# k of chunk 2 loaded in blocks, later attention places and an earlier w_in trigger in a fused retention and GELU kernel

## The chip, the cores and the metric

One core of a Trainium2 chip. The metric is the device time of one execution in microseconds, as the median of several runs. All runs told here are of the fast state; a profile lists one execution, and its span is about 1.7 us shorter than the measured time of the same execution (212.0 against 213.73 for the kernel before).

## The reference, cut to what matters

```python
# q, k, v: (4, 8, 768, 64): batch, head, position, head_dim
for t in range(S):
    state = gamma * state + k[:, :, t] (outer) v[:, :, t]
    y[:, :, t] = 0.125 * q[:, :, t] @ state
x = y.transpose(0, 2, 1, 3).reshape(3072, 512)
h = x @ w_in                      # (512, 2048)
out = gelu_tanh(h) @ w_out        # (2048, 512)
```

The recurrence is computed in six chunks of 128 positions, numbered 0 to 5. In a chunk, for each batch: T (q and k transposed), A (k times q, masked), Y (state times q, plus A times v), S (the new state). The two dense layers of a chunk are called M1 (16 units of TensorE work, then GELU on ScalarE) and M2 (16 units). Attention of chunk n+1 is placed between the units of M1 and M2 of chunk n.

## The kernel before

In the code below PO is GpSimd, VE is VectorE, SY is the SP queue (the DMA queue that SyncE issues), and `prep` scales or converts what was loaded. q of chunks 2 to 5 and k of chunks 3 to 5 are loaded in 32-wide blocks, scaled by GpSimd and transposed by VectorE (0.70 to 0.71 us per 128x512 in the trace of before). All other q and k go through TensorE.

```python
BLK = {"q": (2, 3, 4, 5), "k": (3, 4, 5)}

def load_blk(nm, c):                 # 16 DMAs of 64 KB, runs of 128 bytes
    ...
    for j in range(2):
        for dd in range(2):
            for a in range(4):
                nc.sync.dma_start(out=t[p0:p0 + 32, :, a, :], in_=src[j, dd, t0:t0 + 32])

def load(c):                         # everything of a chunk, on the SP queue
    for nm in "qk":
        if c in BLK[nm]:
            load_blk(nm, c)
    for b in range(B):
        for nm in "vk":              # k also in plain rows: S needs it so
            load1(nc.sync, nm, c, b)

def mm_A(c, b):                      # 8 matmuls; lhsT is k, rhs is q, both transposed
    ...
def ev_A(c, b):                      # 2 masked evictions on VectorE
    ...
```

The start, on GpSimd (`k` of batch 2 is the "third k"):

```python
prep1(PO, "k", 0, 1)
prep1(PO, "k", 0, 2)                 # scale k of batch 2
load_w_in(0)
load_w_in(1)                         # first two w_in parts
prep1(PO, "k", 0, 3)
```

The steady stage, for chunks 3 to 5 (n = c + 1; the keys count units of M1, 0 to 15, and M2, 16 to 31):

```python
after = {
    2: [(prep_blk, nm, n, b) for b in range(B) for nm in "qk"],
    6: [(att_T, n, 0)],
    8: [(att_T, n, 1)] + [(prep1, PO, nm, n, b) for b in range(B) for nm in "kv"],
    9: [(load, n + 1)] if n + 1 < NCk else [],
    10: [(att_T, n, 2)],
    12: [(att_AY, n, (), "att", n, (0, 1), None)],   # A of batches 0 and 1
    14: [(att_T, n, 3)],
    17: [(att_AY, n, (), "att", n, (2, 3), None)],   # A of batches 2 and 3
    21: [(att_Y, n)],
    23: [(att_S, n, 0)], 24: [(att_S, n, 1)], 25: [(att_S, n, 2)], 26: [(att_S, n, 3)],
}
```

Of the kernel before, what the change touches and what calls it, by code (L numbers as in the profile page):

```python
# [9 lines left out]
F16 = mybir.dt.float16  # L10
# [6 lines left out]
def kernel(  # L17
# [9 lines left out]
    nc = tc.nc  # L27
    B, H, S, Dh = q.shape
    C = 128
    NCk = S // C  # L30
    NHP = H // 2
# [25 lines left out]
    pre = ctx.enter_context(tc.tile_pool(name="pre", bufs=2 * B))  # L57
    att = ctx.enter_context(tc.tile_pool(name="att", bufs=4))
# [8 lines left out]
    misc = const.tile([128, 32], F32)  # L67
# [5 lines left out]



    BLK = {"q": (2, 3, 4, 5), "k": (3, 4, 5)}

    def ld_all(key):
        if key not in raw:
            raw[key] = ld.tile(  # L80
                [128, B * NHP, 4, 32],
                F32,
                tag=key[0],
                bufs=2 if key[0] == "q32" else 1,
                name=key[0],
            )
        return raw[key]

    def ld_tile(nm, c, b):
        if nm == "q":  # L90
            t = ld_all(("q32", c)).rearrange("p (b hp) a d -> p b (hp a d)", b=B)
            return t[:, b].rearrange("p (h d) -> p h d", h=H)
        if (nm, c, b) not in raw:
            raw[nm, c, b] = ld.tile([128, H, Dh], F32, tag=f"{nm}32", bufs=6, name=f"{nm}32")
        return raw[nm, c, b]

    def load1(eng, nm, c, b):
        eng.dma_start(  # L98
            out=ld_tile(nm, c, b),
            in_=srcs[nm][b, :, c * C:(c + 1) * C, :].rearrange("h p d -> p h d"),  # L100
        )

    def load_blk(nm, c):
        t = ld_all((nm + ("32" if nm == "q" else "T32"), c))
        src = srcs[nm].rearrange("b (hp j) s (dd d) -> j dd s (b hp) d", j=2, dd=2)
# [3 lines that stand above are left out]
                    p0, t0 = (2 * j + dd) * 32, c * C + a * 32  # L109
                    nc.sync.dma_start(  # L110
                        out=t[p0:p0 + 32, :, a, :], in_=src[j, dd, t0:t0 + 32]
                    )

    def load(c):
# [4 lines that stand above are left out]
            for nm in "vk":  # L119
                load1(nc.sync, nm, c, b)  # L120
# [22 lines left out]
    for j in range(2):  # L143
# [3 lines left out]
        out=iden,  # L147
        in_=iden,
# [7 lines left out]
        out=mask.rearrange("p j hp t -> p (j hp) t"),  # L156
        in_=mask.rearrange("p j hp t -> p (j hp) t"),
# [7 lines left out]
        out=misc[:, 0:1], in_=zero[:, 0:1], func=AF.Gelu_apprx_tanh, scale=1.0  # L165
# [15 lines left out]
    blk16 = {}  # L181

    def prep1(eng, nm, c, b):
        t = pre.tile(
            [128, H, Dh], F16, tag=f"{nm}16", bufs=6 if nm == "q" else 2 * B, name=f"{nm}16"
        )
        src = ld_tile(nm, c, b)
        if nm == "v":
            if eng is nc.scalar:
                eng.copy(out=t, in_=src)  # L190
            else:
                eng.tensor_copy(out=t, in_=src)  # L192
        else:
            col = OQ if nm == "q" else OK
            eng.tensor_tensor(  # L195
                out=t,
                in0=src,
                in1=cst[:, col:col + H].unsqueeze(2).broadcast_to([128, H, Dh]),
                op=ALU.mult,
            )  # L200
        h16[nm, c, b] = t

    def prep_blk(nm, c, b):
        key, tag, col = ("q32", "q16", OQT) if nm == "q" else ("kT32", "kT16", OKT)
        t = pre.tile([128, NHP * 4, 32], F16, tag=tag, bufs=6 if nm == "q" else 2, name=tag)
        nc.gpsimd.tensor_tensor(  # L206
            out=t,
            in0=ld_all((key, c))[:, b * NHP:(b + 1) * NHP].rearrange("p hp a d -> p (hp a) d"),
            in1=cst[:, col:col + 16].unsqueeze(2).broadcast_to([128, 16, 32]),
            op=ALU.mult,  # L210
        )
        blk16[nm, c, b] = t

    def pair(t, hp):
        return t[:, 2 * hp:2 * hp + 2]

    qkT = {}
    a_sb = {}
    xT = {}
    pss = {}  # L220

    def copy_on(eng, out, in_):
        if eng is nc.scalar:
            eng.copy(out=out, in_=in_)  # L224
        else:
            eng.tensor_copy(out=out, in_=in_)  # L226
# [5 lines left out]
    def bank(tag, dt=F32, shape=(128, NHP, 128), name="ps"):  # L232
        return psum.tile(list(shape), dt, tag=tag, bufs=BANKS[tag], name=name)

    def mm_T(c, b):
        parts = [(i, nm) for i, nm in enumerate("qk") if c not in BLK[nm]]
        if not parts:
            return
        ps = bank("att", F16, (128, 2, NHP, 128), "qkT_ps")
        for i, nm in parts:  # L240
            for hp in range(NHP):
                nc.tensor.transpose(  # L242
                    out=ps[:, i, hp], in_=pair(h16[nm, c, b], hp), identity=iden
                )
        pss["T", c, b] = ps

    def ev_T(c, b, eng=nc.vector):
        t = att.tile([128, 2, NHP, 128], F16, tag="qkT", name="qkT")
        for i, nm in enumerate("qk"):
            if c in BLK[nm]:  # L250
                nc.vector.transpose(  # L251
                    out=t[:, i].rearrange("p hp t -> p (hp t)"),
                    in_=blk16.pop((nm, c, b)).rearrange("p ha d -> p (ha d)"),
                )
        if ("T", c, b) in pss:
            i0 = sum(c in BLK[nm] for nm in "qk")
            copy_on(eng, t[:, i0:], pss.pop(("T", c, b))[:, i0:])
        qkT[c, b] = t

    def mm_A(c, b):  # L260
        t = qkT[c, b]
# [90 lines left out]
    def att_T(c, *bs):  # L352
        for b in bs:
            mm_T(c, b)
            ev_T(c, b)
# [51 lines left out]
    def load_w_in(n):  # L407
        i, k0, k1 = w_in_part[n]
        nc.gpsimd.dma_start(  # L409
            out=w_in_sb[n],  # L410
            in_=moe_w_in.rearrange("(kc p) (i n) -> p kc i n", p=128, i=NI)[:, k0:k1, i],
        )
# [29 lines left out]
    def moe1(c, fc):  # L442
        h_ps = bank("h", shape=(128, B * C), name="h_ps")
        moe1_mm(c, fc, h_ps, 0, B * C)
        gelu(g_tile(c, fc)[:, fc % 2], h_ps)
# [65 lines left out]
    def run(units, after):  # L511
        for i, u in enumerate(units):
            u()
            for f, *args in after.get(i, ()):
                f(*args)

    VE, AC, PO, SY = nc.vector, nc.scalar, nc.gpsimd, nc.sync
# [10 lines left out]
    load1(AC, "v", 0, 2)  # L528
    prep1(VE, "q", 0, 1)
    prep1(PO, "k", 0, 1)  # L530
    prep1(PO, "k", 0, 2)

    load_w_in(0)
    load_w_in(1)
    prep1(PO, "k", 0, 3)
    for i in range(2, len(w_in_part)):
        load_w_in(i)
# [97 lines left out]
    )  # L635


    for b in range(B):
        load1(SY, "k", 2, b)
    load_blk("q", 2)  # L640
    for rows, o_sb in late:
        nc.sync.dma_start(out=rows, in_=o_sb)
    for b in range(B):
        load1(SY, "v", 2, b)
    for nm in "kqv":
        for b in range(B):
            prep_blk("q", 2, b) if nm == "q" else prep1(PO, nm, 2, b)
    run(
        [
            (lambda fp=fp, t=t: moe1_two(1, fp, *t))  # L650
# [5 lines left out]
            3: [(att_S, 1, 2)],  # L656
            4: [(att_AY, 1, (3,), "o", 1, (), VE)],
            6: [(att_S, 1, 3)],
            8: [(att_T, 2, 0), (load, 3)],
            10: [(att_T, 2, 1)],  # L660
            14: [(att_AY, 2, (), "att", 2, (0, 1), None)],
        },
    )
    run(
        [x for b in range(B) for x in units2(1, b)],
        {
            0: [(att_T, 2, 2), (att_T, 2, 3)],
            3: [(att_AY, 2, (), "att", 2, (2, 3), None)],
            7: [(att_Y, 2)],
            9: [(att_S, 2, 0)],  # L670
            10: [(att_S, 2, 1)],
            11: [(att_S, 2, 2)],
            12: [(att_S, 2, 3)],
        },
    )

# [1 line left out]
    for c in range(2, NCk - 1):  # L678
        n = c + 1
        after = {  # L680
            2: [(prep_blk, nm, n, b) for b in range(B) for nm in "qk"],
            6: [(att_T, n, 0)],
            8: [(att_T, n, 1)] + [(prep1, PO, nm, n, b) for b in range(B) for nm in "kv"],
            9: [(load, n + 1)] if n + 1 < NCk else [],
            10: [(att_T, n, 2)],
            12: [(att_AY, n, (), "att", n, (0, 1), None)],
            14: [(att_T, n, 3)],
            17: [(att_AY, n, (), "att", n, (2, 3), None)],
            21: [(att_Y, n)],
            23: [(att_S, n, 0)],  # L690
            24: [(att_S, n, 1)],
            25: [(att_S, n, 2)],
            26: [(att_S, n, 3)],
        }
        run(
            [(lambda fc=fc: moe1(c, fc)) for fc in range(NF)]
            + [x for b in range(B) for x in units2(c, b)],
            after,
        )
    c = NCk - 1  # L700
# [36 lines left out]
```

## Time and profile before

| | before |
|---|---|
| time, median of 3 runs | 213.74 us (213.12 to 213.77) |
| span of the profiled run | 212.0 us |
| TensorE busy | 204.6 us, 96% |
| TensorE waits after 18.2 us | none |
| matmuls that transpose q or k | 80 |

The page, TensorE's waits and the chain are shown in the prediction. One more view is needed later: the order of loads on the SP queue, which is never idle from 65 to 94 us. The columns are start, duration of the issue, engine queue, line, operation, what, count. The last line is GpSimd scaling the first k block of chunk 3.

```profile
65.04 9.93 SPq L110 DMA_DIRECT2D q<-in_q_dram  x16
75.03 8.77 SPq L110 DMA_DIRECT2D kT<-in_k_dram  x16
...
88.39 1.05 POOL L206 TENSOR_TENSOR kT<-kT,cst 128x512 f16<-128x512 f32 x1
```

The k blocks of chunk 3 were all issued by 83.8 us (the last landed at 86.40), and GpSimd came to them at 88.39 without waiting. A of chunk 3 stood at 96.86, so they were ready far ahead.

### The profile page before, as it was taken

How to read it: one execution, taken by the hardware profiler on the slowest of the kernel's cores; microseconds unless marked ns; L12 is line 12 of the kernel's file. 1: busy time of each engine (PE TensorE's matmuls, PEld its weight loads, DVE VectorE, ACT ScalarE, POOL GpSimd, SP SyncE). 2: the span in 40 equal slices, each digit the busy share in tenths (PEclk: the TensorE clock that was granted, in tenths of full speed). 3: DMA queues.
4: the chain of work that ended last, by engine and by line, in shares of the span. 5: the costliest groups of instructions: out<-in, count | busy, mean ns of one | idle time of the engine just before them, and what ended most of it. 6: DMA issues, size and time to landing. Idle time of an engine off the chain costs nothing.

```text
span 212.0 us, 3873 instructions
## 1 busy us (share of the span) xinstructions
PE 204.6 (96%) x1518; PEld 111.1 (52%) x1518; DVE 89.6 (42%) x162; ACT 84.2 (40%) x141; POOL 94.8 (45%) x116
## 2 busy tenths in 40 slices
PE   7798999999999999999999999999999999999992
PEld 2457444457897465444465444464444464444461
DVE  6677100198618736356544356544356520100000
ACT  2464661255455131466131466131466131565110
POOL 2597300523819517799218699211699201100000
PEclk9999999999999999999999999999999999999999
DMA  6999999999889878998779996799900012100121
GB/s 155 289 251 206 206 203 231 233 246 236 135 229 215 148 170 134 250 222 148 120 154 205 290 183 108 122 186 254 248 0 3 0 49 102 49 0 0 49 102 50
DMA packets 124289, 32.78 MB, mean 155 GB/s; under 512 B 118064, under 2 KB 122416, under 8 KB 124272
## 3 DMA queue, kind: packets, MB, share of 16 engines
q1 hardware_dynamic: 108880, 20.75, 49.5%
q0 software_dynamic: 5600, 8.65, 17.1%
q10 hardware_dynamic: 9792, 3.15, 6.2%
q8 instruction: 12, 0.20, 0.4%
q14 instruction: 5, 0.04, 0.1%
HBM read 30.44 MB, written 6.29 MB: 173 GB/s over the span
## 4 chain that ended last, share of the span: by engine, by line
PE 90%; DMA 7%; POOL 1%; SPq 1%; DVE 0%; issue 0%
PE o_ps L470 40%; PE h_ps L425 39%; DMA w_in<-in_moe_w_in_dram 3%; DMA k<-in_k_dram 3%; PE a_ps L265 3%; PE y_ps L300 3%; PE y_ps L287 2%; PE s_ps L319 2%; PE qkT_ps L242 1%; SPq L98 1%; POOL k L195 0%; POOL w_in L409 0%; DVE o_sb L508 0%; SPq L126 0%
## 5 line engine op out<-in xcount | busy, mean ns | idle before, releaser
L470 PE MATMUL o_ps<-w_out,g 128*128 128x512 f16 (+1 forms) x400 | 88.2, 371 | 0.0
L425 PE MATMUL h_ps<-xT,w_in 128*128 128x512 f16 (+1 forms) x464 | 86.6, 343 | 0.7 <-DMA w_in<-in_moe_w_in_dram 0.7
L440 ACT ACTIVATE g<-h_ps 128x512 f16<-128x512 f32 x96 | 57.3, 597 | 48.2 <-PE h_ps L425 48.1
L425 PEld LDWEIGHTS <-w_in 128*128 128x128 f16 x464 | 44.4, 98 | 38.1 <-DMA w_in<-in_moe_w_in_dram 0.8
L470 PEld LDWEIGHTS <-g 128*128 128x128 f16 x400 | 37.6, 98 | 38.7
L278 DVE TENSOR_TENSOR a_sb<-a_ps,mask 128x512 f16<-128x512 f32 x48 | 30.1, 683 | 17.5 <-PE a_ps L265 17.5
L492 ACT COPY o_sb<-o_ps 128x512 f32<-128x512 f32 x19 | 11.1, 585 | 54.9 <-PE o_ps L470 50.5
L497 POOL DMA_DIRECT2D out_dram<-o_sb x17 | 9.6, 563 | 47.3 <-ACT o_sb L492 37.5
L195 POOL TENSOR_TENSOR k<-k,cst 128x512 f16<-128x512 f32 x23 | 23.7, 1035 | 12.3 <-DMA k<-in_k_dram 12.3
L345 POOL TENSOR_TENSOR stg<-st,cst 128x512 f32<-128x512 f16 x16 | 16.4, 1040 | 10.7 <-DVE st L336 8.9
L206 POOL TENSOR_TENSOR q<-q,cst 128x512 f16<-128x512 f32 x16 | 16.6, 1047 | 5.0 <-DMA out_dram<-o_sb 5.0
L336 DVE TENSOR_TENSOR st<-s_ps,stg 64x256 f16<-64x256 f32 x32 | 13.5, 421 | 7.8 <-PE s_ps L319 7.3
L251 DVE STREAM_TRANSPOSE qkT<-q 128x512 f16<-128x512 f16 x16 | 11.3, 707 | 11.6 <-POOL q L206 11.6
L195 DVE TENSOR_TENSOR q<-q,cst 128x512 f16<-128x512 f32 x8 | 5.9, 739 | 16.0 <-DMA q<-in_q_dram 15.9
L226 DVE CAST xT<-y_ps 128x512 f16<-128x512 f32 x11 | 7.2, 686 | 12.7 <-PE y_ps L300 12.7
L206 POOL TENSOR_TENSOR kT<-kT,cst 128x512 f16<-128x512 f32 x12 | 12.5, 1042 | 0.0
L508 DVE COPY o_sb<-o_ps 128x256 f32<-128x256 f32 x2 | 0.8, 424 | 26.6 <-PE o_ps L470 26.6
L224 ACT CAST xT<-y_ps 128x512 f16<-128x512 f32 x13 | 7.2, 587 | 8.7 <-PE y_ps L300 8.7
L171 PE MATMUL spin_ps<-zero 128*128 128x512 f16 x30 | 9.1, 444 | 1.3 <-DVE zero L139 1.3
L490 DVE COPY o_sb<-o_ps 128x512 f32<-128x512 f32 x4 | 2.8, 691 | 16.4 <-PE o_ps L470 14.7
L251 DVE STREAM_TRANSPOSE qkT<-kT 128x512 f16<-128x512 f16 x12 | 8.4, 700 | 2.6 <-POOL kT L206 2.6
L192 POOL CAST v<-v 128x512 f16<-128x512 f32 x16 | 9.5, 602 | 0.0
(33 smaller groups left out, 97.5 us busy)
## 6 DMA issues: line engine op xcount, KB each, us to landing
v<-in_v_dram SPq DMA_DIRECT2D x22, 256.0 KB, 4.4
k<-in_k_dram SPq DMA_DIRECT2D x20, 256.0 KB, 4.7
out_dram<-o_sb POOLq DMA_DIRECT2D x17, 256.0 KB, 3.2
q<-in_q_dram SPq DMA_DIRECT2D x64, 64.0 KB, 2.6
kT<-in_k_dram SPq DMA_DIRECT2D x48, 64.0 KB, 2.6
w_out<-in_moe_w_out_dram POOLq DMA_DIRECT2D x4, 512.0 KB, 15.8
w_in<-in_moe_w_in_dram POOLq DMA_DIRECT2D x3, 512.0 KB, 9.2
q<-in_q_dram SPq DMA_DIRECT2D x5, 256.0 KB, 5.9
```

What stands on the lines that cost most here:

```text
L192: eng.tensor_copy(out=t, in_=src)
L195: eng.tensor_tensor(out=t, in0=src, in1=cst[:, col:col + H].unsqueeze(2).broadcast_to([128, H, Dh]), op=ALU.mult,)
L206: nc.gpsimd.tensor_tensor(out=t, in0=ld_all((key, c))[:, b * NHP:(b + 1) * NHP].rearrange("p hp a d -> p (hp a) d"), in1=cst[:, col:col + ...
L251: nc.vector.transpose(out=t[:, i].rearrange("p hp t -> p (hp t)"), in_=blk16.pop((nm, c, b)).rearrange("p ha d -> p (ha d)"),)
L278: nc.vector.tensor_tensor(out=s, in0=ps[j], in1=mask[:, j], op=ALU.mult)
L336: eng.tensor_tensor(out=st[sl, :, b, sl], in0=s_ps[sl, :, sl], in1=stg[sl, :, b, sl], op=ALU.add,)
L345: nc.gpsimd.tensor_tensor(out=stg[:, :, b], in0=st[:, :, b], in1=cst[:, OG:OG + NHP].unsqueeze(2).broadcast_to([128, NHP, 128]), op=ALU.mult,)
L425: nc.tensor.matmul(out=out, lhsT=w_in_of(fc, kc), rhs=xT[c][:, kc, t0:t1], start=(kc == 0 and first), stop=(kc == NHP - 1), skip_group_che ...
L440: nc.scalar.activation(out=out, in_=in_, func=AF.Gelu_apprx_tanh, scale=1.0)
L470: nc.tensor.matmul(out=ps[:, n0:n1], lhsT=g_sb[c, fc // 2][:, fc % 2, b * C:(b + 1) * C], rhs=w_out_sb[fc // (NF // NO)][:, fc % (NF // NO ...
L492: nc.scalar.copy(out=o_sb, in_=ps)
L497: eng.dma_start(out=rows, in_=o_sb)
```

## The change

Three things: k of chunk 2 also comes in blocks, so that no TensorE transposes are left after chunk 1; attention of chunks 2 to 5 is placed later, with all q transposed well ahead of k; and w_in is triggered as soon as the third k has landed, before it is scaled. To hold the first two apart, `tr` (the transposes on VectorE) now runs for q and for k separately, GpSimd scales all four q blocks before the four k blocks, and there are four buffers for scaled k blocks instead of two; these lines are not shown.

```diff
-    BLK = {"q": (2, 3, 4, 5), "k": (3, 4, 5)}
+    BLK = {"q": (2, 3, 4, 5), "k": (2, 3, 4, 5)}
@@ start
     prep1(PO, "k", 0, 1)
-    prep1(PO, "k", 0, 2)
+    nc.gpsimd.tensor_copy(out=misc[0:1, 4:5], in_=ld_tile("k", 0, 2)[0:1, 0, 0:1])
     load_w_in(0)
     load_w_in(1)
+    prep1(PO, "k", 0, 2)
     prep1(PO, "k", 0, 3)
@@ loads of chunk 2
-    for b in range(B):
-        load1(SY, "k", 2, b)
     load_blk("q", 2)
+    load_blk("k", 2)
     ...
+    for nm in "vk":
         for b in range(B):
+            load1(SY, nm, 2, b)
+    load(3)
@@ M2 of chunk 1 (keys: units; chunk 2's A used to be at unit 14 of M1 and 3 of M2)
+            1: [(tr, 2, "k", 0, 1)],
+            3: [(att_AY, 2, (), "att", 2, (0, 1), None), (tr, 2, "k", 2, 3)],
+            7: [(att_AY, 2, (), "att", 2, (2, 3), None)],
+            11: [(att_Y, 2)],
+            12: [(att_S, 2, 0)],   ... 15: [(att_S, 2, 3)],
@@ chunks 3 to 5
-            12: A(0, 1)   14: T(3)   17: A(2, 3)   21: Y   23 to 26: S        (shortened)
+            2: [(prep, n, "QKvk"), (tr, n, "q")],
+            15: [(tr, n, "k", 0, 1)],
+            18: [(att_AY, n, (), "att", n, (0, 1), None), (tr, n, "k", 2, 3)],
+            22: [(att_AY, n, (), "att", n, (2, 3), None)],
+            26: [(att_Y, n)],
+            27: [(att_S, n, 0)],   ... 30: [(att_S, n, 3)],
```

More of the change, by code (lines that the diff above doesn't have):

```diff
@@ L204, in prep_blk @@
         key, tag, col = ("q32", "q16", OQT) if nm == "q" else ("kT32", "kT16", OKT)
-        t = pre.tile([128, NHP * 4, 32], F16, tag=tag, bufs=6 if nm == "q" else 2, name=tag)
+        t = pre.tile([128, NHP * 4, 32], F16, tag=tag, bufs=6 if nm == "q" else 4, name=tag)
         nc.gpsimd.tensor_tensor(
@@ L235, in mm_T @@
     def mm_T(c, b):
-        parts = [(i, nm) for i, nm in enumerate("qk") if c not in BLK[nm]]
-        if not parts:
-            return
         ps = bank("att", F16, (128, 2, NHP, 128), "qkT_ps")
-        for i, nm in parts:
+        for i, nm in enumerate("qk"):
             for hp in range(NHP):
@@ L245, in mm_T, with qkT_tile, tr @@
         pss["T", c, b] = ps
+    def qkT_tile(c, b):
+        if (c, b) not in qkT:
+            qkT[c, b] = att.tile([128, 2, NHP, 128], F16, tag="qkT", name="qkT")
+        return qkT[c, b]
     def ev_T(c, b, eng=nc.vector):
-        t = att.tile([128, 2, NHP, 128], F16, tag="qkT", name="qkT")
-        for i, nm in enumerate("qk"):
-            if c in BLK[nm]:
-                nc.vector.transpose(
-                    out=t[:, i].rearrange("p hp t -> p (hp t)"),
-                    in_=blk16.pop((nm, c, b)).rearrange("p ha d -> p (ha d)"),
-                )
-        if ("T", c, b) in pss:
-            i0 = sum(c in BLK[nm] for nm in "qk")
-            copy_on(eng, t[:, i0:], pss.pop(("T", c, b))[:, i0:])
-        qkT[c, b] = t
+        copy_on(eng, qkT_tile(c, b), pss.pop(("T", c, b)))
+    def tr(c, nm, *bs):
+        for b in bs or range(B):
+            nc.vector.transpose(
+                out=qkT_tile(c, b)[:, "qk".index(nm)].rearrange("p hp t -> p (hp t)"),
+                in_=blk16.pop((nm, c, b)).rearrange("p ha d -> p (ha d)"),
+            )
     def mm_A(c, b):
@@ L635, with prep @@
     )
-    for b in range(B):
-        load1(SY, "k", 2, b)
     load_blk("q", 2)
+    load_blk("k", 2)
     for rows, o_sb in late:
         nc.sync.dma_start(out=rows, in_=o_sb)
-    for b in range(B):
-        load1(SY, "v", 2, b)
-    for nm in "kqv":
+    for nm in "vk":
         for b in range(B):
-            prep_blk("q", 2, b) if nm == "q" else prep1(PO, nm, 2, b)
+            load1(SY, nm, 2, b)
+    load(3)
+    def prep(c, nms):
+        for nm in nms:
+            for b in range(B):
+                prep1(PO, nm, c, b) if nm in "kv" else prep_blk(nm.lower(), c, b)
     run(
@@ L658 @@
             6: [(att_S, 1, 3)],
-            8: [(att_T, 2, 0), (load, 3)],
-            10: [(att_T, 2, 1)],
-            14: [(att_AY, 2, (), "att", 2, (0, 1), None)],
+            7: [(prep, 2, "Q")],
+            8: [(tr, 2, "q")],
+            10: [(prep, 2, "Kvk")],
         },
@@ L666 @@
         {
-            0: [(att_T, 2, 2), (att_T, 2, 3)],
-            3: [(att_AY, 2, (), "att", 2, (2, 3), None)],
-            7: [(att_Y, 2)],
-            9: [(att_S, 2, 0)],
-            10: [(att_S, 2, 1)],
-            11: [(att_S, 2, 2)],
-            12: [(att_S, 2, 3)],
+            1: [(tr, 2, "k", 0, 1)],
+            3: [(att_AY, 2, (), "att", 2, (0, 1), None), (tr, 2, "k", 2, 3)],
+            7: [(att_AY, 2, (), "att", 2, (2, 3), None)],
+            11: [(att_Y, 2)],
+            12: [(att_S, 2, 0)],
+            13: [(att_S, 2, 1)],
+            14: [(att_S, 2, 2)],
+            15: [(att_S, 2, 3)],
         },
@@ L680 @@
         after = {
-            2: [(prep_blk, nm, n, b) for b in range(B) for nm in "qk"],
-            6: [(att_T, n, 0)],
-            8: [(att_T, n, 1)] + [(prep1, PO, nm, n, b) for b in range(B) for nm in "kv"],
+            2: [(prep, n, "QKvk"), (tr, n, "q")],
             9: [(load, n + 1)] if n + 1 < NCk else [],
-            10: [(att_T, n, 2)],
-            12: [(att_AY, n, (), "att", n, (0, 1), None)],
-            14: [(att_T, n, 3)],
-            17: [(att_AY, n, (), "att", n, (2, 3), None)],
-            21: [(att_Y, n)],
-            23: [(att_S, n, 0)],
-            24: [(att_S, n, 1)],
-            25: [(att_S, n, 2)],
-            26: [(att_S, n, 3)],
+            15: [(tr, n, "k", 0, 1)],
+            18: [(att_AY, n, (), "att", n, (0, 1), None), (tr, n, "k", 2, 3)],
+            22: [(att_AY, n, (), "att", n, (2, 3), None)],
+            26: [(att_Y, n)],
+            27: [(att_S, n, 0)],
+            28: [(att_S, n, 1)],
+            29: [(att_S, n, 2)],
+            30: [(att_S, n, 3)],
         }
```

## The prediction

> **What bounds the kernel now.** I read four views in this order: the page's busy rows and slices, the waits of TensorE alone, the chain of work that ended last, and the timelines of TensorE and VectorE around one attention block.
>
> From the page:
>
> ```profile
> PE 204.6 (96%) x1518; PEld 111.1 (52%) x1518; DVE 89.6 (42%) x162; ACT 84.2 (40%) x141; POOL 94.8 (45%) x116
> ...
> PE   7798999999999999999999999999999999999992
> ...
> PEclk9999999999999999999999999999999999999999
> ```
>
> TensorE is busy at full granted clock from the fifth slice (about 21 us) to the end, and no other engine reaches half. Busy TensorE is not proof, since ends of matmuls are modelled, so the next view is who TensorE waited for:
>
> ```profile
> PE a_ps L265 <- ACT qkT L224: 1.3, 3, 0.6
> PE spin_ps L171 <- DVE zero L139: 1.3, 1, 1.3
> PE h_ps L425 <- DMA w_in<-in_moe_w_in_dram: 0.7, 1, 0.7
> ```
>
> These three rows are all there is. All lie in the first 18.2 us; afterwards TensorE waits for nothing. So after 18 us only two things change the time: matmuls removed, at their issue spacing, and new waits. The chain (start, duration, what) shows the spacing and where the start-up ends:
>
> ```profile
> 2.36 6.42 DMA k<-in_k_dram
> 8.78 0.07 issue
> 8.85 1.04 POOL k L195
> 9.89 0.84 POOL w_in L409
> 10.72 7.36 DMA w_in<-in_moe_w_in_dram
> 18.09 0.05 issue
> 18.14 0.61 PE h_ps L425 x4
> ...
> 60.65 0.22 PE qkT_ps L242 x4
> ...
> 62.62 0.22 PE qkT_ps L242 x4
> ...
> 68.74 0.45 PE qkT_ps L242 x8
> 69.18 2.59 PE o_ps L470 x12
> ```
>
> The start-up is third k lands, GpSimd scales it, GpSimd triggers w_in, w_in lands at 18.09, first full-rate work. Later, four transposes take 0.22 us of TensorE (55 ns each) and four 512-column matmuls 2.59/3 = 0.863 us (216 ns each).
>
> [...] I count removed work at the spacing, not at the 219 ns that the groups give as the mean of one 128-column matmul. [...] the trace shows the vector form at 0.70 us per 128x512. [...] the DMA share in the slices is 9 throughout from 5 to 53 us. [...] 1 MB of q in 32-wide blocks (128 B runs) took the SP queue 9.59 us, 1 MB of k in plain rows (256 B runs) 4.66 us.
>
> **The change part by part.**
>
> *k of chunk 2 in blocks.* Removes 4 batches x 4 = 16 TensorE transposes: 16 x 55 ns = 0.88 us, all on the setting path (the rows above: 0.22 + 0.22 + 0.45 = 0.89). It also removes 4 PSUM copies of about 0.40 us on VectorE and adds 4 vector transposes of 0.70 us, 4 GpSimd multiplies of 1.04 us and 1 MB of block loads, about 9 us of SP queue. None of those is on the path unless late. *Gain 0.88 us.*
>
> *Later attention.* Moves no work in or out of TensorE, the same matmuls run a few units later. It only matters through waits. The critical distance is between the two A groups: in the before loop there were 5 units between them, now 4. From the timelines of chunk 3:
>
> ```profile
> 96.86 0.62 PE L265 MATMUL a_ps<-qkT 64*128 64x128 f16 x16
> ...
> 97.29 2.48 DVE L278 TENSOR_TENSOR a_sb<-a_ps,mask 128x512 f16<-128x512 f32 x4 [3.09 <-PE a_ps L265]
> 99.69 0.70 DVE L251 STREAM_TRANSPOSE qkT<-q 128x512 f16<-128x512 f16 x1
> 100.31 0.67 DVE L251 STREAM_TRANSPOSE qkT<-kT 128x512 f16<-128x512 f16 x1
> ```
>
> VectorE starts evicting 0.43 us after A starts, needs 2.48 us for four evictions, then 0.62 us per transpose pitch: the second one ends 4.12 us after A's start (100.98 - 96.86). In the changed loop the two k transposes of batches 2 and 3 stand exactly there. TensorE comes back for batch 2 after 0.55 + 4 x 0.865 + 0.11 (the small lag seen after each A group) = 4.12 us and for batch 3 at about 4.39. Batch 2 is ready at about 3.5, batch 3 at 4.12. So the wait is nil, but batch 3 has only some 0.25 us to spare. *Expected 0 to 0.1 us for each of four chunks; I put 0.1 in all.*
>
> *Loads of chunk 2.* SP starts q blocks at 44.65 instead of k's plain rows: q until 54.3, k blocks (9 us) until about 63.5, landing 2.6 us later, about 66. GpSimd then needs 2 x 1.04 us and VectorE 0.70 us until batch 1's k is transposed: 69. M2 of chunk 1 begins at 67.87 - 0.55 (A moved out) - 0.44 (transposes) = 66.9 and A of chunk 2 follows 4 units later, at 70.3. Slack a bit over 1 us. Afterwards all loads are some 9 us later in the SP queue: chunk 3's loads end at about 102 instead of 93.6. Its v is first read by TensorE at unit 26, about 109, and GpSimd's last v conversion is due at about 104. Later chunks regain 3.5 us each (stage 31.8 us, loads 28.3 us). *0, or a wait of up to 1 us once.*
>
> *w_in earlier.* GpSimd now does a 1x1 copy instead of the 1.04 us multiply ahead of the trigger (the only 1x1 copy in the trace took 0.18 us), so w_in is triggered about 0.85 us earlier. But the k multiply of batch 2 comes after two triggers of together 1.64 us: it ends at about 11.7 instead of 9.89. TensorE transposed that k at 11.14, so the batch-2 chain slips about 0.5 us. Following it through (transpose, PSUM copy, A, eviction, last y) the last y before the w_in wait ends at about 17.9 instead of 17.48. It waited for w_in until 18.14. So even a w_in that lands 0.85 us earlier gives only 18.14 - 17.9 = 0.25 us. If the DMA engines are simply full, w_in lands at 18.1 as before and the gain is 0. *Gain 0.15 us.*
>
> Sum: 0.88 + 0.15 - 0.1 = 0.93, say 1.0 us with the three before runs lying at 213.12 to 213.77: 213.74 - 1.0 = 212.7 us.
>
> **The rivals.** (a) *A new wait takes the gain back*: k transposes of batches 2 and 3 queue behind the evictions on VectorE. For it: the distance of 4 units leaves only 0.25 us. Against: the before durations, taken from the same overlap with GpSimd, just fit. With 0.3 us of lateness in each of four chunks it would cost 1.2 us: 213.7, no change. (b) *Chunk 2's k blocks land late.* For it: DMA shares of 9 from 44 to 52 us, SP never pausing. Against: slack over 1 us. It costs as much as it is late: 213 to 214. (c) *The start-up gains more*: if w_in's landing sets all and the k slip is absorbed by the dummy (spin) matmuls, it gains 0.65 us (the whole TensorE wait), total 212.2. For it: TensorE does run 3 dummies right after that transpose. Against: those dummies are in program order and are pushed back too. (d) *The start-up loses*: the slip exceeds 0.65 us, and the time is 0.2 to 0.5 us worse than I say.
>
> **Range and chances.** The transposes are nearly certain (-0.88). Start-up: -0.65 to +0.4. Waits: 0 to +1.2. Run to run: about 0.3. I take 211.9 to 213.9. A gain or loss of 2% is 4.3 us. A gain that large isn't there: total start-up before 18.14 us would have to shrink by a fifth. A loss that large needs a DMA wait of over 5 us, or one in each stage; 2%. So faster 0.01, same 0.97, slower 0.02.
>
> **What would show it.** In the changed profile: the transposes on TensorE drop from 80 to 64 matmuls and vector transposes rise from 28 to 32. The chain has no transposes between 60 and 69 us. TensorE's waits show no new row after 19 us; a row of A waiting for the vector transposes is rival (a) if in every chunk, (b) if only in chunk 2 near 70 us. The first row of w_in's chain starts near 9.0 us; w_in landing near 18.1 means the DMA engines were full, near 17.3 that the trigger set it; the idle time before that matmul should fall from 0.65 us to below 0.3. I am wrong if TensorE idles anywhere in M1 or M2, if the first full-rate matmuls start outside 17.5 to 18.5 us, or if the time moves more than 2 us.

## The result, and the profile after

The changed kernel took 212.5 us in the median of 4 runs (211.97 to 212.62), against 213.75 for the kernel before. The ratio is 0.9943, with a 95% interval of 0.9917 to 0.9969. Ratios here are the mean time of one kernel's fast runs over that of the other's fast runs of the same rounds, so they are not quite the ratio of the medians that stand beside them.

The lines that answer to those of before: the page, TensorE's waits, and the chain.

```profile
PE 203.5 (97%) x1502; PEld 110.3 (52%) x1502; DVE 91.4 (43%) x162; ACT 84.3 (40%) x141; POOL 100.0 (48%) x121
```

```profile
PE a_ps L264 <- ACT qkT L224: 1.3, 3, 0.6
PE spin_ps L171 <- DVE zero L139: 1.3, 1, 1.3
PE qkT_ps L239 <- POOL k L195: 0.4, 1, 0.4
```

```profile
8.60 0.18 POOL misc L532
8.78 1.60 POOL w_in L408 x2
10.38 1.08 POOL k L195
...
11.51 0.40 PE qkT_ps L239 x4
...
17.80 0.54 PE h_ps L424 x4
...
58.50 7.86 PE h_ps L424 x72
```

The 16 matmuls are gone (1518 to 1502), the vector transposes rise from 28 to 32, the stretch from 58.5 us holds only M1 work where two groups of transposes stood, and nothing waits after 19 us. In the start the wait for w_in has been replaced by a wait for the third k, the slip that the prediction described (last y until 17.80, foreseen 17.9, before 17.48), and the first full-rate work stands at 17.80 in the chain (17.73 in the timeline) instead of 18.14.

Following the chain from mark to mark says where the time between the two traces went. The M1 that follows the start begins its main part at 21.60 before and 21.19 after (0.41 us). The last matmul ends at 208.05 and 206.75 (1.30 us). So 0.89 us fell between these two marks, and the transposes are 0.88 by count. The remaining 0.4 us of the 1.7 us by which the spans differ lies after the last output has landed (210.24 and 208.93 us, 2.2 us after the last TensorE work in both), at the end of the program, which no part of the change touches.

That reading makes everything look settled: 0.89 for the transposes, 0.41 for the start. But two traces are two draws, and the profiled run of the changed kernel was the fastest of its four (211.97 us). One view of the changed kernel warned that it is close to an edge. The SP queue, then GpSimd, VectorE and TensorE around A of chunk 3:

```profile
74.56 11.47 SPq L110 DMA_DIRECT2D q<-in_q_dram  x16
86.14 9.43 SPq L110 DMA_DIRECT2D kT<-in_k_dram  x16
...
97.90 4.07 POOL L206 TENSOR_TENSOR kT<-kT,cst 128x512 f16<-128x512 f32 x4 [4.98 <-DMA kT<-in_k_dram]
...
99.99 0.71 DVE L254 STREAM_TRANSPOSE qkT<-kT 128x512 f16<-128x512 f16 x1 [0.30 <-POOL kT L206]
...
100.74 0.62 PE L264 MATMUL a_ps<-qkT 64*128 64x128 f16 x16
101.17 2.48 DVE L277 TENSOR_TENSOR a_sb<-a_ps,mask 128x512 f16<-128x512 f32 x4 [0.47 <-PE a_ps L264]
103.57 1.30 DVE L254 STREAM_TRANSPOSE qkT<-kT 128x512 f16<-128x512 f16 x2
...
104.85 0.62 PE L264 MATMUL a_ps<-qkT 64*128 64x128 f16 x16
```

GpSimd now waits 4.98 us for the k blocks of chunk 3. k of batch 1 is transposed at 99.99 + 0.71 = 100.70, and TensorE begins A at 100.74 with batch 0 and comes to batch 1 at 100.97: some 0.2 us to spare, since TensorE starts about 0.06 us after a transpose that it waited for (in d3 below, transposed at 105.50 and A at 105.56). The later pair shows the same for VectorE: the transposes of batches 2 and 3 end at 104.87, and A of batch 2 begins at 104.85, that of batch 3 at 105.09.

### The profile page after: what moved, and what is told of

Read it like the earlier page. It is cut to its first block, busy times and chain, and to the rows that moved or that the text cites. A ratio compares the mean times of both kernels' runs of the same rounds, so it can differ in the third digit from the quotient of the medians.

```text
span 210.3 us, 3858 instructions
## 1 busy us (share of the span) xinstructions
PE 203.5 (97%) x1502; PEld 110.3 (52%) x1502; DVE 91.4 (43%) x162; ACT 84.3 (40%) x141; POOL 100.0 (48%) x121
## 4 chain that ended last, share of the span: by engine, by line
PE 92%; DMA 3%; POOL 1%; ACT 1%; SPq 1%; DVE 0%; issue 0%
PE o_ps L469 40%; PE h_ps L424 40%; PE y_ps L299 3%; DMA k<-in_k_dram 3%; PE a_ps L264 3%; PE y_ps L286 2%; PE s_ps L318 2%; PE qkT_ps L239 1%; POOL w_in L408 1%; PE spin_ps L171 1%; POOL k L195 1%; SPq L98 1%; ACT qkT L224 0%; ACT v L190 0%; DVE o_sb L507 0%
## 5 line engine op out<-in xcount | busy, mean ns | idle before, releaser
L424 PE MATMUL h_ps<-xT,w_in 128*128 128x512 f16 (+1 forms) x464 | 85.6, 342 | 0.0
L277 DVE TENSOR_TENSOR a_sb<-a_ps,mask 128x512 f16<-128x512 f32 x48 | 30.2, 684 | 17.9 <-PE a_ps L264 17.8
L344 POOL TENSOR_TENSOR stg<-st,cst 128x512 f32<-128x512 f16 x16 | 16.4, 1039 | 12.6 <-DVE st L335 10.7
L206 POOL TENSOR_TENSOR kT<-kT,cst 128x512 f16<-128x512 f32 x16 | 16.3, 1050 | 10.7 <-DMA kT<-in_k_dram 10.2
L254 DVE STREAM_TRANSPOSE qkT<-kT 128x512 f16<-128x512 f16 x16 | 10.9, 698 | 13.3 <-POOL kT L206 13.3
L264 PE MATMUL a_ps<-qkT 64*128 64x128 f16 x192 | 8.1, 218 | 1.3 <-ACT qkT L224 1.3
```

The source lines that it names most:

```text
L206: nc.gpsimd.tensor_tensor(out=t, in0=ld_all((key, c))[:, b * NHP:(b + 1) * NHP].rearrange("p hp a d -> p (hp a) d"), in1=cst[:, col:col + ...
L254: nc.vector.transpose(out=qkT_tile(c, b)[:, "qk".index(nm)].rearrange("p hp t -> p (hp t)"), in_=blk16.pop((nm, c, b)).rearrange("p ha d - ...
L264: nc.tensor.matmul(out=ps[j][:, hp], lhsT=t[j * 64:(j + 1) * 64, 1, hp], rhs=t[j * 64:(j + 1) * 64, 0, hp], start=True, stop=True,)
L277: nc.vector.tensor_tensor(out=s, in0=ps[j], in1=mask[:, j], op=ALU.mult)
L344: nc.gpsimd.tensor_tensor(out=stg[:, :, b], in0=st[:, :, b], in1=cst[:, OG:OG + NHP].unsqueeze(2).broadcast_to([128, NHP, 128]), op=ALU.mult,)
L424: nc.tensor.matmul(out=out, lhsT=w_in_of(fc, kc), rhs=xT[c][:, kc, t0:t1], start=(kc == 0 and first), stop=(kc == NHP - 1), skip_group_che ...
```

## The experiments

Twelve kernels ran, in three sets, each set on one chip with its own runs of the kernel before. All gave correct results. Times are medians of 5 or 6 runs.

| kernel | us | before in the same set | ratio, 95% interval |
|---|---|---|---|
| s1, trigger alone | 213.45 | 213.71 | 0.9988 [0.9976, 1.0000] |
| s2, all but the trigger | 213.35 | 213.71 | 0.9985 [0.9968, 1.0001] |
| s3, later places alone | 213.24 | 213.71 | 0.9980 [0.9969, 0.9991] |
| s4, blocks at the early places | 218.57 | 213.71 | 1.0225 [1.0205, 1.0245] |
| r, changed kernel again | 213.12 | 213.57 | 0.9971 [0.9947, 0.9995] |
| d3, three units between A groups | 215.23 | 213.57 | 1.0080 [1.0061, 1.0098] |
| w2, third k scaled between the triggers | 213.30 | 213.57 | 0.9986 [0.9964, 1.0007] |
| w3, w_in not held | 213.82 | 213.57 | 1.0035 [1.0007, 1.0064] |
| b1, more slack | 212.11 | 213.30 | 0.9950 [0.9930, 0.9970] |
| b2, more slack, old start | 212.56 | 213.30 | 0.9957 [0.9937, 0.9977] |
| control, the kernel before | 213.74 | 213.30 | 1.0022 [1.0001, 1.0044] |
| r2, changed kernel a third time | 213.03 | 213.30 | 0.9986 [0.9969, 1.0003] |

The control belongs at the head of any reading. The kernel before, measured against itself, came out at 1.0022 with an interval that leaves out 1. So a difference of about 0.5 us between two kernels, in one set, may be nothing at all.

### The changed kernel again (r and r2)

No edit.

> The changed kernel once more, for a second trace. In the first one k of chunk 3 was transposed 0.1 us before TensorE needed it (100.70 against 100.81). Theory A: no wait of TensorE after 19 us in this trace either, 212.5 us. Rival: the slack is a matter of luck, this trace has a wait of A for the vector transposes near 100 us of 0.1 to 0.6 us.

> The changed kernel a third time, beside the version with slack. Theory A: k blocks of chunk 3 start to be scaled between 97.8 and 99.3 us; if after 98.0, A of chunk 3 waits, by up to 1.2 us in all; median 212.5 to 213.1. Rival: no wait, and as fast as the version with slack.

The rival of the first expectation held. In the trace of r (the SP queue, GpSimd, TensorE with its two waits):

```profile
74.30 12.64 SPq L110 DMA_DIRECT2D q<-in_q_dram  x16
87.05 9.56 SPq L110 DMA_DIRECT2D kT<-in_k_dram  x16
...
99.20 4.07 POOL L206 TENSOR_TENSOR kT<-kT,cst 128x512 f16<-128x512 f32 x4 [5.00 <-DMA kT<-in_k_dram]
...
101.06 0.40 PE L264 MATMUL a_ps<-qkT 64*128 64x128 f16 x8 [0.27 <-DVE qkT L254]
102.06 0.40 PE L264 MATMUL a_ps<-qkT 64*128 64x128 f16 x8 [0.61 <-DVE qkT L254]
```

The q blocks took the queue 12.64 us instead of 11.47, the k blocks behind them were scaled 1.3 us later, and TensorE waited twice. What it cost is read from the distance between the first M1 matmul of chunk 2 and that of chunk 3: 31.85 us in the first trace (84.24 to 116.09), 32.97 in r (84.22 to 117.19), 32.39 in r2 (84.78 to 117.17), which had one wait of 0.36 us. So 1.12 and 0.54 us were lost, more than the idle time of 0.88 and 0.36, because idle time is counted from the modelled end of the last matmul, and the next can be issued before that (one 128-column matmul is shown as 0.22 us long, though the chain has four of them in 0.22 us). The same loss comes out from the other side: in r A of batch 1 began 1.11 us later after the start of M1 than in the first trace (17.84 against 16.73 us), in r2 0.53 us later (17.26). In r that is more than the 16 transposes had brought. The first result was the luckier draw: 0.9943, then 0.9971 and 0.9986, which average 0.9967, or some 0.7 us.

### More slack, with the new start and with the old (b1 and b2), and the control

```diff
 # M2 of chunk 1: chunk 2 one unit later
-            1: tr k(0, 1)   3: A(0, 1)   7: A(2, 3)   11: Y   12, 13, 14, 15: S
+            2: tr k(0, 1)   4: A(0, 1)   8: A(2, 3)   12: Y   13, 14, 15, 15: S
 # chunk 3 only: two units later
-            15: tr k(0, 1)  18: A(0, 1)  22: A(2, 3)  26: Y   27, 28, 29, 30: S
+            17: tr k(0, 1)  20: A(0, 1)  24: A(2, 3)  28: Y   29, 30, 31, 31: S
```

b2 has, on top, the start order of the kernel before (third k scaled, then the two triggers).

> The changed kernel with attention of chunk 2 one unit later and of chunk 3 two units later (1.7 us). Theory A (in the second trace of the changed kernel TensorE lost the gain of the transposes again because k blocks of chunk 3 were scaled from 99.2 us on instead of 97.9, and needed from 98.0): no wait of TensorE after 19 us in the trace, and steadily 0.9 to 1.2 us faster than before; faster than the changed kernel in the same call by 0.3 to 0.8 us. Rival (the spread of the changed kernel is something else, such as the start or the clock): same time and spread as the changed kernel.

> The version with more slack, with the start-up order of before. Theory A (the w_in part is worth little on the mean: the first second-layer matmul stood at 31.80, 31.35 and 31.00 us in three traces with the old order and at 31.31 to 31.44 in five with the new): within 0.2 us of the version with slack and the new order, 0.9 us faster than before. Theory B (w_in part worth the 0.4 us of the first pair of traces): 0.4 us slower than the version with slack.

> The kernel before as a kernel of its own, for a second trace and as a control: ratio 1.000 within 0.002. Theory A (the late w_in of the first trace, landing 18.1 us, was one draw): w_in's second part lands near 16.7 us and TensorE does not wait for it. Theory B: it lands near 18 again.

TensorE's waits in b1:

```profile
PE spin_ps L171 <- DVE zero L139: 1.3, 1, 1.3
PE a_ps L264 <- ACT qkT L224: 1.1, 3, 0.5
PE qkT_ps L239 <- POOL k L195: 0.4, 1, 0.4
```

No wait after 19 us, although the k blocks of chunk 3 were scaled from 98.60 us on, late enough for the changed kernel to lose time (97.90 with 0.2 us to spare put its limit near 98.1). The distance from chunk 2's M1 to chunk 3's is 31.85 us again. By the ratios b1 is 0.0036, or 0.77 us, faster than the changed kernel in the same set (medians 212.11 and 213.03), within what the expectation gave. The two differ only in these places, and r2's trace lost 0.54 us to chunk 3 where b1's lost none. 0.77 us is more than the 0.5 us that the control showed for no change, though not by much; the traces are the firmer evidence. Against the kernel before b1 is clearly ahead (0.9930 to 0.9970). Its trace keeps some 1.5 us of slack for chunk 3 (k of batch 1 transposed at 100.69 + 0.71 = 101.40, its A at 102.95).

b2 ran 0.0007 (0.15 us) behind b1, well inside the intervals: the w_in part is worth little. The control's trace bears that out: the second w_in part landed 6.1 us after its trigger, and TensorE did not wait for it. That it landed late in the first trace of before (7.4 us) was a draw. More telling is when it landed. In the four other traces with the old order it was triggered at 10.53 to 10.68 us and landed at 16.58 to 16.75; with the change's order (first trace, r, r2, s1, b1) it was triggered at 9.61 to 9.92 and landed at 16.55 to 16.95. Triggering it some 0.9 us earlier did not bring it in earlier.

### The trigger alone, and all but the trigger (s1 and s2)

```diff
 # s1: the kernel before, with                  # s2: the changed kernel, with
     prep1(PO, "k", 0, 1)                           prep1(PO, "k", 0, 1)
-    prep1(PO, "k", 0, 2)                       -    1x1 copy waiting for the third k
+    1x1 copy waiting for the third k           +    prep1(PO, "k", 0, 2)
     load_w_in(0)                                   load_w_in(0)
     load_w_in(1)                                   load_w_in(1)
+    prep1(PO, "k", 0, 2)                       -    prep1(PO, "k", 0, 2)
```

> The kernel before with the w_in part of the change alone: a 1x1 copy that waits for the third k, then two w_in triggers, then the scaling of that k. Theory A (the two gains simply add: start-up about 0.4 us as in the two traces, transposes 0.89 us): 0.3 to 0.4 us faster than before, about 213.4; the second w_in part lands near 16.5 us instead of 18.1, and TensorE does not wait for it. Rival B (the earlier start of the changed kernel's trace was run-to-run variation in when k landed, the DMA engines are full anyway): 0 to 0.1 us faster, w_in near 18 us. Rival C (the delayed k costs more than w_in gives): slower than before.

> The changed kernel with the start-up order of before. Theory A: only the 16 transposes are gone, 0.89 us faster than before, about 212.85, and about 0.35 us slower than the changed kernel; TensorE waits about 0.6 us for w_in again. Rival B: as fast as the changed kernel, 212.5.

s1 was 0.26 us faster than before, with an interval that reaches from 0.5 to 0: between theory A and rival B. s2 was 0.3 us faster than before instead of the 0.89 expected of theory A: its trace has the same waits as r, of A, 0.17 us in chunk 2 and 0.61 us in chunk 3. By the distance from one M1 to the next they cost 0.34 and 0.88 us, more than the transposes had brought.

Why the start is worth so little shows when the starts of all traces are laid side by side: the length of the first run of 14 dummy matmuls, which ends before the first transposes, and where the first work behind the last y begins (marked w where it waited for w_in).

| old order: dummies, then | new order: dummies, then |
|---|---|
| 4.66 us, 17.34 (s3) | 4.63 us, 17.73 (changed) |
| 4.84 us, 18.14 w (before) | 4.74 us, 17.70 (r) |
| 5.46 us, 17.69 (s2) | 4.61 us, 17.72 (s1) |
| 6.00 us, 18.23 (b2) | 5.05 us, 17.98 (b1) |
| 6.01 us, 18.25 (control) | 5.91 us, 18.27 (r2) |

With short dummies and w_in in time (s3 alone), the old order is 0.35 us better, because the new one makes TensorE wait 0.4 us for the third k. With w_in late (one of five), the new order is 0.4 us better. With long dummies both are alike. The dummies' length is the clock: 14 matmuls of 512 columns would take 3.0 us at the 216 ns that the chain shows later, and the first ones are issued 0.43 us apart, twice that. In the traces' own clock records nothing is recorded before the first stretch of full clock (`prof` prints 1.00 there), and this stretch begins between 4.05 and 6.99 us (4.62 in the first trace of before, 4.21 in that of the changed kernel), in each trace where the spacing halves, or at the last dummy where all 14 are slow. So its beginning does not keep a fixed distance from the start of the kernel: the first dummy is issued at 1.25 to 1.26 us in all 14 traces, and the 14 take from 4.55 to 6.01 us. The recorded stretches of full clock last 64.85, 143.36, 204.80 or 208.21 us, each a whole multiple of 3.413 us (19, 42, 60 and 61 times). What sets their beginning no run shows.

### Later places alone (s3)

```diff
 # the kernel before, T at its old places
-            chunk 2: A at 14 of M1 and 3 of M2, Y at 7, S at 9 to 12
+            chunk 2: A at 3 and 7 of M2, Y at 11, S at 12 to 15
-            chunks 3 to 5: A at 12 and 17, Y at 21, S at 23 to 26
+            chunks 3 to 5: A at 18 and 22, Y at 26, S at 27 to 30
```

> The kernel before with only the places of attention moved later as in the change; k of chunk 2 still goes through TensorE, loads and scalings as before. Theory A (places move no work and no wait): within 0.1 us of before, 213.75. Rival (later places are worth time by themselves, or cost it through a wait of TensorE for the vector transposes): 0.4 us or more away from before, with a new row among the waits of TensorE.

The trace agrees with theory A: no new wait, and from the first M2 to the M1 of the last chunk it took 148.51 us (31.00 to 179.51) against 148.40 before (31.80 to 180.20). The time does not quite: 0.4 us faster than before. Its profiled run had one of the fastest starts (dummies 4.66 us), but why its six runs together should be faster is not settled; it is no more than what the control showed against itself.

### Blocks at the early places (s4)

```diff
 # the changed kernel, places of the kernel before
-            chunk 2: A at 3 and 7 of M2, Y 11, S 12 to 15
+            chunk 2: tr k at 10 of M1, A at 14 of M1 and 3 of M2, Y 7, S 9 to 12
-            chunks 3 to 5: tr k 15, A 18 and 22, Y 26, S 27 to 30
+            chunks 3 to 5: tr k 10, A 12 and 17, Y 21, S 23 to 26
```

> The changed kernel with attention of chunks 2 to 5 back at the old places. Theory A (the later places are what lets the 1 MB of k blocks of chunk 2 land in time): from the changed kernel's trace k of chunk 2 is transposed for two batches at 69.1 us, and A at the old place would stand at 65.5, so TensorE waits about 3.4 us; in chunk 3 it is 100.7 against 99.1 after that shift, about 1.4 us more; later none. Sum 4.8 us slower than the changed kernel, about 217.3. Rival (slack was ample, as the prediction had it for chunk 3; places don't matter): 212.5 to 213.

Theory A held: without later places the blocks are a loss of 4.9 us against before. TensorE's new wait row (us in total, times, longest):

```profile
PE a_ps L264 <- DVE qkT L254: 5.1, 4, 3.6
```

The same kernel in stretches, during the first wait and behind it (stretch, its length, busy time of PE, PEld, DVE, ACT and POOL with counts, then the granted clock, DMA share, GB/s):

```profile
66.00:68.00 2.00, 0.00 (x0) 0.00 (x0) 0.00 (x0) 0.18 (x1) 0.67 (x1) 1.00 0.99 305
...
72.00:73.00 1.00, 1.00 (x5) 0.57 (x4) 1.00 (x3) 0.35 (x1) 0.50 (x1) 0.50 1.11 251
```

The waits are 3.63 and 0.61 us in chunk 2 and 0.24 and 0.61 in chunk 3: 5.1 us, where 4.8 were expected. The time rose more than that, because behind the wait of 3.63 us TensorE ran at half clock until about 73 us: the wait lasted from 65.54 to 69.17 us, and the clock record shows half clock from 69.69 to 73.10 us. That the wait brought the half clock on is the author's estimate, from their order in this one trace. The second wait fell into it until 70.18, so some 2.9 us of work ran at half speed, about 1.4 us on top. The distances from M1 to M1 agree: 5.85 and 1.09 us longer than in the first trace of the changed kernel, 6.9 us in all.

### Three units between the A groups (d3)

```diff
-            7: A(2, 3) of chunk 2       22: A(2, 3) of chunks 3 to 5
+            6: A(2, 3) of chunk 2       21: A(2, 3) of chunks 3 to 5
```

> The changed kernel with three units of TensorE work between the two A groups of chunks 2 to 5 instead of four. Theory A (VectorE's four evictions and two transposes set the distance: the second transpose ends 4.1 us after A starts, TensorE would be back for batch 3 after about 3.5): a wait of 0.55 to 0.6 us in each of four chunks, 2.3 us slower than the changed kernel, 214.8. Rival (the distance has more slack than the trace says): below 0.5 us slower.

It was 0.0109 of the time, or 2.3 us, behind the changed kernel of the same set. That is the number of theory A, in part by luck: r itself lost time in chunk 3. From M1 to M1 the trace lost 0.71 us in each of the four chunks, not 0.55 to 0.6, or 2.8 us in all. Each of the four chunks shows the pair of waits; chunk 3's, with VectorE:

```profile
101.81 2.48 DVE L277 TENSOR_TENSOR a_sb<-a_ps,mask 128x512 f16<-128x512 f32 x4 [0.92 <-PE a_ps L264]
104.21 1.29 DVE L254 STREAM_TRANSPOSE qkT<-kT 128x512 f16<-128x512 f16 x2
...
104.97 0.40 PE L264 MATMUL a_ps<-qkT 64*128 64x128 f16 x8 [0.28 <-DVE qkT L254]
105.56 0.40 PE L264 MATMUL a_ps<-qkT 64*128 64x128 f16 x8 [0.20 <-DVE qkT L254]
```

So the distance of four units of the change is the smallest that doesn't wait.

### Two more orders of the start (w2 and w3)

```diff
 # w2                                   # w3
     1x1 copy waiting for the third k   -    1x1 copy waiting for the third k
     load_w_in(0)                            load_w_in(0)
-    load_w_in(1)                            load_w_in(1)
     prep1(PO, "k", 0, 2)                    prep1(PO, "k", 0, 2)
+    load_w_in(1)
```

> The changed kernel with the scaling of the third k between the two w_in triggers. Theory A (after the change the start is set by TensorE's late k of batch 2, not by w_in): TensorE no longer waits 0.4 us for that k; if the second w_in part still lands by 17.3 us, 0.3 us faster than the changed kernel, 212.2. Rival B (what counts is that both triggers come early): the second part lands near 18 again and the gain of the start-up is lost, 212.8.

> The changed kernel without the 1x1 copy: w_in is triggered when the second k has been scaled, near 7.1 us, 1.6 us earlier still. Theory A [...]: w_in's first two parts land about 1 us earlier, but third k, q and v of batches 2 and 3 land later by up to 1 us, and TensorE's chain with them: 0 to 0.5 us slower than the changed kernel. Rival B [...]: nothing lands later, TensorE does not wait for the scaled k of batch 2, 0.3 us faster, 212.2.

In w2 TensorE did not wait for the third k, as theory A said, but there was no gain: its trace has dummies of 5.65 us, and VectorE's scaling of the next q took 1.25 us instead of 0.69, while GpSimd scaled k (the columns are start, duration, engine, operation):

```profile
10.16 1.25 DVE L195 TENSOR_TENSOR q<-q,cst 128x512 f16<-128x512 f32 x1
...
9.80 1.05 POOL L195 TENSOR_TENSOR k<-k,cst 128x512 f16<-128x512 f32 x1
```

The added 0.56 us is close to the 0.69 us by which the two scalings overlap; that the overlap caused it is the author's estimate, and no run took it away. Whether the dummies or the slower scaling kept w2 from gaining is left open: the medians are within what the control shows. There is a third candidate that this trace cannot show, waits in chunk 3 as in r: its profiled run had none and was the fastest of the six (212.39 us, median 213.30).

w3 was slower, as its theory A said. w_in was triggered from 6.90 us on, while loads of chunk 0 were still to land, and its second part landed at 15.45 us, 1.1 us earlier than in the changed kernel's first trace; v of batch 2 landed 9.5 us after its issue instead of 6.2, and the chain waited for it:

```profile
PE y_ps L299 <- ACT v L190: 1.7, 1, 1.7
```

## Why the prediction was right or wrong

The time, the range and the class were right: 212.7 predicted, 212.5 measured. The closeness is partly luck: two later measurements of the same kernel gave 213.12 and 213.03, with gains of 0.6 and 0.3 us. By its steps:

- *16 transposes, 0.88 us.* Right. 0.89 us between the marks of the two traces, and 0.9 to 1.1 us by runs in the two versions that have no waits (b1 and b2, ratios 0.9950 and 0.9957).
- *Distance of four A units, 0 to 0.1 us per chunk.* Right: no wait. The margin was somewhat smaller than the 0.25 us that it gave to batch 3: the trace shows 104.87 against 105.09, and d3 lost 0.71 us per chunk when one unit of 0.865 us was taken away, which leaves 0.15 us.
- *w_in earlier, 0.15 us.* Right in size (0.26 us in s1, 0.15 us between b1 and b2, neither clear of noise) and in the slip of the third k, which became the wait that the trace shows. Its two signs, landing near 17.3 or near 18.1, both failed: w_in landed at 16.57. The 18.1 was the draw of one trace. But its case for no gain, that an earlier trigger does not land earlier, is what the nine traces above show; that full DMA engines are the reason is argued, not tested.
- *Loads of chunk 2, "0, or a wait of up to 1 us once".* The size was right, the place was wrong, and this is the step that failed. It gave chunk 2's k blocks a slack "a bit over 1 us", and of chunk 3 it checked only that v, first read at 109, would be there by 104. It did not check chunk 3's k blocks, which are read from 100.8 us on. Its own figures (chunk 3's loads some 9 us later than the 65.04 us of before, 9.6 us of q blocks, 9 of k blocks, 2.6 to landing) put them near 95 us, and some 3 us for scaling and transposing the first two make 98: still about 3 us of slack. What used it up was the queue, which took longer than in the trace before. In the three traces of the changed kernel the q blocks began at 74.3 to 76.4 us and took 10.8 to 12.6 us, so the k blocks were issued from 86.1 us at the earliest and took 9.4 to 9.6 us; they were scaled from 97.9 to 99.2 us on, and A needed that to begin by about 98.1 (98.6 in r2, which started later). So it waited in two of three traces, at a cost of 1.12 and 0.54 us. This was rival (b), in chunk 3 instead of 2; chunk 2 waited only in s2, 0.17 us, and had 0.8 us to spare in the first trace (k of batch 1 ready at 69.13, its A at 69.98).
- *Nothing idles in M1 or M2*, said to be what would prove it wrong: true in the trace that came with the result, false in the next two. On the average of three measurements the gain was some 0.7 us, not 1.25.
- *Short runs.* It sets side by side how long 16 DMAs with runs of 128 B and 4 DMAs with runs of 256 B occupied the SP queue (9.59 and 4.66 us). Number and run length of the DMAs changed together, so this does not show the cost of short runs.

Shown: the waits of chunk 3 and their cost (r, r2), and that a later place removes them (b1). Only argued: why the queue ran late; v and plain k of chunk 2 stand directly ahead of the q blocks and are still landing, but no run took these away. Nor is it one thing: in r the q blocks took 12.64 us, in r2 10.79, but there they began 1.8 us later than in the first trace.

## What to carry to other kernels

When work moves off the bound engine onto a transfer, follow every later consumer of that queue, not only the data that was moved: here 1 MB added for chunk 2 made chunk 3's blocks late. A slack of 0.2 us in one trace is a wait in the next one, so profile the same kernel twice before explaining tenths of a microsecond, and measure the kernel before against itself. Where there is freedom to place work later at no cost, take a microsecond of slack: the moved units of b1 brought nearly as much (0.77 us) as the transposes (0.88 us).

## Figures that these traces give

- A group of four 128x128 transposes on TensorE takes 0.22 us of the chain, 55 ns each (before, at 60.65 and 62.62 us); the record of one shows 219 ns. A saving reckoned from the record would be four times too large. (The trace lists them as MATMUL.)
- On VectorE a transpose of 128x512 in one instruction takes 0.71 us, and 0.62 us from one to the next, or 155 to 178 ns per 128x128 (before, at 99.69 and 100.31 us, and the changed kernel).
- 1 MB in 16 DMAs with runs of 128 B occupies the SP queue for 8.8 us (before) to 12.6 us (r), 1 MB in 4 DMAs with runs of 256 B for 3.8 us (b2) to 5.0 us (r2), and in this kernel the time at which a block could be issued in that queue decided when k was there.
- With the first dummy at 1.25 to 1.26 us in every trace, the first stretch of full clock began between 4.05 and 6.99 us, a range of 2.9 us; the first full-rate work moved with it, by 0.6 us with the change's order of the start (17.70 to 18.27) and by 0.9 us with the old one (17.34 to 18.25).
